# Two token pairs projected from centred rows, loads in another order, and a new order of all steps

## The chip, the cores and the metric

The kernel runs on one core of a Trainium2 chip. The metric is the device time of one execution in microseconds (us), lower is better. The kernel before took 153.5 us (median of 3 runs, 153.39 to 153.69). The profile is of one further execution of 153.96 us.

## The reference, cut to what matters

The input x has 2048 tokens of 448 features. It is layer-normed once, and two branches that read the result are added to x:

```python
xn = _layernorm(x)                       # (x - mean) / sqrt(var + 1e-5), no weights
return x + _A_ref(xn, ...) + _B_ref(xn, ...)

# A: linear attention with a softmax feature map, 16 heads of 28
q, k, v = split(xn @ wqkv)
phi(t) = concat[softmax(t @ w_phi), softmax(-(t @ w_phi))]        # per head, 56 features
kv = sum_s phi(k)^T v ;  z = sum_s phi(k)
o  = (phi(q) @ kv) / (phi(q) @ z + 1e-6) ;  A = o @ wo
# B: feed-forward, 448 -> 1792 -> 448
h = xn @ w1 + b1 ;  B = (h * tanh(softplus(h))) @ w2
```

The norm's scale, 1/sqrt(var + eps), is one number for each token, so a projection of x - mean can be scaled by it afterwards.

## The kernel before, in words

**Tiling.** 2048 tokens are 16 tiles of 128 (t = 0 to 15), and two tiles make a pair u (0 to 7). A pair's normed rows are transposed into xnT (features on partitions); 448 features are three chunks of 128 and one of 64, and the 64 of both tiles share a chunk. `pair_part` splits a projection of a pair into three parts of matmuls on half the array's rows: A (6), B (6) and H (2). A pair of PSUM banks is held from a step's first part to the end of its evacuation; there are four pairs.

**Stages.** Loads; statistics of each tile (`st`, on VectorE by bn_stats, on ScalarE by three activations); the rstd (`rt`, `rs`); normed rows (`xn`, `ln_tile`); their transposes (`xt`, on TensorE or as a DMA transpose in SP's queue). The weights of k and q are first multiplied with w_phi: `wtk` transposes the k weights on TensorE and evacuates them to WT, `wmk` multiplies them to Wpk; the q weights come already transposed by four DMA transposes (`lqT`), `qd` doubles their last 64 columns on VectorE, and `wmq` multiplies them to Wpq. For each pair there is then a k, v and q projection (L429 for all). ScalarE takes exp of k and of q with both signs (L609, L682); v is copied out by ScalarE or VectorE (L509, L511). `kn` normalizes k's features (a sum and a reciprocal on VectorE, a multiplication on GpSimd, L621). `kv` (L650) sums over all pairs, and `kvz` sends the result through a DMA transpose. `e` turns exp(q) of a tile by a DMA transpose in SP's queue, `nd` (L723) makes numerator and denominator, `ot` turns the quotient, `wo` (L845) projects it. The feed-forward is `f` (L429, with Mish on ScalarE, L703) and `g` (L828). VectorE adds x, and the rows are stored.

**What sets the order.** A list of step names, ORDER, written out by hand. `run_order` calls the steps in that order, and each appends its instructions to its engines' programs. So an engine runs its instructions strictly in list order, and an instruction that waits holds up all behind it on that engine, a DMA in SP's or ScalarE's queue too. `resolve` puts in the semaphore waits. `warm` (`z`) issues matmuls of zeros.

Of the kernel before, what the change touches and what calls it, by code (L numbers as in the profile page):

```python
# [38 lines left out]
class Program:  # L39
# [113 lines left out]
v6Aa xn11p kn0.1 k6H v6Ha k3A kn0.0 xt5m kn1.1 l1ms k6A v3Ad kc3 k6B v3Hd k7A v3Bd k7H v4Hd kn6.0 e3 v4Ad k7B v4Bd k4B
v7Ba k4H k4A e2 k5B kn7.1 v7Aa kn7.0 q4H k5A v7Ha kc2 e0 k5H q4A e5 f0.0B q4B f0.0H v5Bd f0.0A e9 f0.8H f0.8A v5Ad
kn5.0 f0.3B f0.8B v5Hd f0.3A e1 f0.4B f0.3H e8 q3B f0.4A f0.5A f0.4H f0.5H f0.2H f0.2A kn1.0 f0.5B kn4.1 q5H e4 q5A
f0.2B q3H kn6.1 loa q7B q5B q7A q7H kn5.1 kn4.0 kv2 kv6 ep kv1 kv0 kv5 kv7 kv4 kv3 q3A f1.0B kvz f0.9A e10 f1.0A f1.0H
e14 f0.9H e15 f0.6A f0.9B f0.7B f0.6H nd0 f0.7A f0.6B f0.11H f0.11A f0.7H f0.10B nd3 f0.11B f0.12A f0.10A e11 e6
f0.10H nd1 f0.12H e7 ot0m f0.1B f0.12B f0.1A f0.1H q6A q6H f1.13H nd2 q6B f1.5A f1.13A f1.4A f1.13B f1.5H f1.1H f1.1A
f1.4B f1.1B f1.5B f1.6A f1.6H e12 f1.4H ot1m f1.11A f1.6B f1.11B nd4 f1.12H f1.11H l2s f1.12A f0.13B f1.12B f1.7A nd5
f1.7H f0.13H f0.13A f1.2H f1.7B ot2m f1.2A nd7 wo0H f1.2B wo1B wo0A wo1A nd6 ot3m wo1H wo0B nd10 g2 g7 g3 g1 g0 nd12  # L160
e13 f1.10A f1.10H f1.9A f1.9H wo3B f1.10B nd13 f1.9B wo3A wo3H f1.8B ot6m f1.3H nd11 f1.3A ot5m g6 g5 f1.8H nd15 f1.8A
wo2H f1.3B sto1 wo2B nd14 nd9 wo2A nd8 g4 sto3 g14 g9 sto2 g12 ot7m g8 ot4m g13 wo7H wo4B wo7A wo5A wo6A wo5H wo6H
# [9 lines left out]
def _kernel(es, nc, A_x, A_wqkv, A_w_phi, A_wo, B_w1, B_b1, B_w2, out):  # L172
    def sb(name, shape, dtype):
        return es.enter_context(nc.sbuf_tensor(name, shape, dtype))
# [108 lines left out]

    def load_qT(g, eng):
        dma(eng, lambda e: e.dma_start_transpose(WqT[:, g, 0:D], A_wqkv[:, g * GP:g * GP + P]), w=[("WqT", g)],
# [618 lines left out]
    add("kvz", kvz)
    add("wob", last_weights)
    add("table", table)
    for eng, c in (("SP", "s"), ("ACT", "a")):
        for a in range(NT):
            for b in range(a + 1, NT + 1):
                add(f"lx{a}.{b}{c}", load_x, a, b, eng)  # L910
        for i, (n, t) in enumerate((("k", Wk), ("v", Wv))):
            add(f"l{n}m{c}", load_main, eng, "W" + n, t, A_wqkv[:, (i + 1) * D:(i + 2) * D])
        add(f"lkt{c}", load_tail, eng, "Wkv", Wkv, A_wqkv[:, D:3 * D])
# [66 lines left out]
```

## Time and profile before

| | us |
|---|---|
| median of 3 runs | 153.5 |
| the profiled execution | 153.96 |
| its span | 152.2 |
| outside the span | 1.76 |
| TensorE busy in the span | 144.6 |
| VectorE, ScalarE, GpSimd busy | 101.1, 75.7, 44.3 |

The page gives the busy time of each engine, the span in 40 slices, and the chain of work that ended last. The timeline gives single instructions with their start and duration; instructions of a group overlap, so a group of n can be shorter than n single ones. "Us to landing" of a DMA is from its issue until its data is there.

### The profile page before, as it was taken

How to read it: one execution, taken by the hardware profiler on the slowest of the kernel's cores; microseconds unless marked ns; L12 is line 12 of the kernel's file. 1: busy time of each engine (PE TensorE's matmuls, PEld its weight loads, DVE VectorE, ACT ScalarE, POOL GpSimd, SP SyncE). 2: the span in 40 equal slices, each digit the busy share in tenths (PEclk: the TensorE clock that was granted, in tenths of full speed). 3: DMA queues.
4: the chain of work that ended last, by engine and by line, in shares of the span. 5: the costliest groups of instructions: out<-in, count | busy, mean ns of one | idle time of the engine just before them, and what ended most of it. 6: DMA issues, size and time to landing. Idle time of an engine off the chain costs nothing.

```text
span 152.2 us, 3611 instructions
## 1 busy us (share of the span) xinstructions
PE 144.6 (95%) x1541; PEld 76.1 (50%) x1541; DVE 101.1 (66%) x223; ACT 75.7 (50%) x90; POOL 44.3 (29%) x65
## 2 busy tenths in 40 slices
PE   3978999989999979999999999999999999999993
PEld 1454545445444574445344455554544554559552
DVE  0699989599969903599606999535995999200721
ACT  3485999995995699778997730000500400000000
POOL 3385688969999950000000000000000000000000
PEclk9999999999999999999999999999999999999999
DMA  5995964989967243994399260500035000540204
GB/s 123 288 260 147 174 143 93 131 268 262 101 137 138 76 139 73 180 197 41 60 149 321 86 65 14 119 0 0 2 65 151 30 4 0 121 121 4 87 4 151
DMA packets 40436, 17.22 MB, mean 113 GB/s; under 512 B 34020, under 2 KB 39908, under 8 KB 40420
## 3 DMA queue, kind: packets, MB, share of 16 engines
q1 hardware_dynamic: 37548, 14.46, 46.9%
q10 hardware_dynamic: 2872, 2.53, 5.6%
q8 instruction: 12, 0.20, 0.5%
q14 instruction: 4, 0.03, 0.1%
HBM read 7.02 MB, written 1.84 MB: 58 GB/s over the span
## 4 chain that ended last, share of the span: by engine, by line
PE 78%; ACT 12%; DMA 4%; DVE 3%; issue 1%; ACTq 0%
PE PS L429 38%; PE PS L828 28%; PE PS L845 7%; DMA x_all<-in_A_x_dram 4%; ACT actT L609 3%; PE PS L723 2%; PE PS L650 2%; ACT actT L682 2%; ACT v_all L509 2%; DVE Sk L627 1%; ACT Wpq L509 1%; ACT Eq L682 1%; DVE v_all L511 1%; ACT Eq L509 1%; ACT Wpk L509 1%
## 5 line engine op out<-in xcount | busy, mean ns | idle before, releaser
L703 ACT ACTIVATE actT<-PS,b1T 128x1024 bf16<-128x1024 f32 x28 | 30.2, 1112 | 33.1 <-PE PS L429 33.0
L429 PE MATMUL PS<-xnT,W 64*128 64x512 bf16 x392 | 46.2, 376 | 0.0
L828 PE MATMUL PS<-W,actT 128*128 128x448 bf16 (+1 forms) x224 | 42.7, 351 | 0.0
L828 PEld LDWEIGHTS PS<-W,actT 128*128 128x128 bf16 x224 | 21.5, 98 | 20.3 <-issue 0.7
L429 PEld LDWEIGHTS PS<-xnT,W 64*128 64x128 bf16 x392 | 18.1, 94 | 21.0 <-ACT actT L703 0.4
L793 DVE TENSOR_TENSOR x_all<-PS,x_all 128x448 bf16<-128x448 f32 (+1 forms) x16 | 9.5, 616 | 20.3 <-PE PS L845 10.3
L621 POOL TENSOR_TENSOR actT<-actT,rSk 128x896 bf16<-128x896 bf16 x12 | 20.0, 1699 | 0.0
L609 ACT ACTIVATE actT<-PS 128x896 bf16<-128x896 f32 x16 | 13.7, 950 | 3.7 <-DVE stats L466 1.8
L429 PE MATMUL PS<-Wkv,xnT 64*128 64x448 bf16 x112 | 13.6, 349 | 0.6 <-DVE v_all L511 0.6
L429 PE MATMUL PS<-Wpk,xnT 64*128 64x448 bf16 x112 | 13.3, 349 | 0.5 <-ACT Wpk L509 0.5
L429 PE MATMUL PS<-Wpq,xnT 64*128 64x448 bf16 x112 | 12.7, 350 | 0.0
L466 DVE BATCH_NORM_STATS2 stats<-x_all 128x6 f32<-128x448 bf16 x15 | 9.2, 614 | 5.2 <-DMA x_all<-in_A_x_dram 5.2
L617 DVE TENSOR_REDUCE Sk<-actT 128x32 f32<-128x896 bf16 x12 | 12.5, 1043 | 0.0
L738 DVE COPY Sq<-PS 128x16 f32<-128x16 f32 x32 | 4.0, 167 | 12.5 <-PE PS L723 12.2
L749 DVE TENSOR_TENSOR xn<-v_all,rden 128x448 bf16<-128x448 f32 x16 | 10.0, 625 | 1.3 <-DMA Wkv<-xn 0.8
L746 DVE TENSOR_TENSOR v_all<-v_all 128x464 f32<-128x464 f32 x16 | 10.3, 642 | 0.6
L742 DVE TENSOR_TENSOR v_all<-PS,Sq 128x464 f32<-128x464 f32 x16 | 10.3, 642 | 0.5
L744 DVE TENSOR_TENSOR v_all<-PS,Sq 128x464 f32<-128x464 f32 x16 | 10.1, 630 | 0.0
L429 PEld LDWEIGHTS PS<-Wkv,xnT 64*128 64x128 bf16 x112 | 5.4, 94 | 6.0 <-DVE v_all L511 1.0
L682 ACT ACTIVATE actT<-PS 128x896 bf16<-128x896 f32 x10 | 8.4, 926 | 0.0
L429 PEld LDWEIGHTS PS<-Wpk,xnT 64*128 64x128 bf16 x112 | 5.3, 94 | 5.5 <-ACT Wpk L509 0.6
L429 PEld LDWEIGHTS PS<-Wpq,xnT 64*128 64x128 bf16 x112 | 5.1, 94 | 5.4 <-ACT actT L609 0.5
(85 smaller groups left out, 137.7 us busy)
## 6 DMA issues: line engine op xcount, KB each, us to landing
W<-in_B_w_dram SPq DMA_DIRECT2D x1, 1568.0 KB, 8.0
out_dram<-x_all SPq DMA_DIRECT2D x7, 224.0 KB, 2.2
W<-in_B_w_dram SPq DMA_DIRECT2D x1, 1344.0 KB, 7.2
x_all<-in_A_x_dram ACTq DMA_DIRECT2D x5, 224.0 KB, 4.1
Wo<-in_A_wo_dram ACTq DMA_DIRECT2D x2, 336.0 KB, 3.6
x_all<-in_A_x_dram SPq DMA_DIRECT2D x2, 224.0 KB, 4.9
W<-in_B_w_dram SPq DMA_DIRECT2D x2, 224.0 KB, 4.0
Wkv<-in_A_wqkv_dram SPq DMA_DIRECT2D x1, 336.0 KB, 4.2
```

The lines of the kernel that those rows point to most:

```text
L429: ins = e.matmul(o, lhs(c, k), rhs(c, k), start=first and n == at[par][0], stop=last and n == at[par][-1])
L609: op("ACT", lambda e, s=s: e.activation(E_of(u)[:, s, :, :], two(b, D), ACT.Exp, scale=1.0 if s == 0 else -1.0), r=[pb(b), pb(b + 1)], w=[ ...
L617: op("DVE", lambda e: e.tensor_reduce(Sk[u][:, s, :], Eh(), AX.X, ALU.add), r=[("E", u, s)], w=[("Sk", u, s)], tag=f"Sk{u}.{s}")
L621: op("POOL", lambda e: e.tensor_tensor(Eh(), Eh(), ap_on(rSk[u][:, s, 0:1], [[1, 2 * H], [0, DH]]), ALU.mult), r=[("E", u, s), ("rSk", u, ...
L682: op("ACT", lambda e, s=s: e.activation(Eq_of(u)[:, :, s, :].rearrange("p i (h n) -> p i h n", n=64)[:, :, :, 0:QP], two(b, D).rearrange(" ...
L703: op("ACT", lambda e: e.activation(actT[:, q, fc, :], bank(b, 2), ACT.Mish, bias=b1T[:, fc:fc + 1]), r=[("b1T",), pb(b), pb(b + 1)], w=[(" ...
L742: op("DVE", lambda e: e.tensor_tensor(tv(t1[i]), num(0), sx(1), ALU.mult), r=[pb(b), pb(b + 1), ("Sq", i, 1)], w=[("t1", i)], tag=f"ta{t}")
L744: op("DVE", lambda e: e.tensor_tensor(tv(t2), num(1), sx(0), ALU.mult), r=[pb(b), pb(b + 1), ("Sq", i, 0)], w=[("t2",)], tag=f"tb{t}")
L746: op("DVE", lambda e: e.tensor_tensor(t1[i], t1[i], t2, ALU.add), r=[("t1", i), ("t2",)], w=[("t1", i)], tag=f"tc{t}")
L749: op("DVE", lambda e: e.tensor_tensor(o_sb[(t // 2) % 2][:, t % 2, :].rearrange("p (h d) -> p h d", d=DH), t1[i][:, :, 0:DH], ap_on(rden[i ...
L828: ins = e.matmul(bank(b)[:, 0:width(t)], act_of(fc, t), W2[:, fc, 0:width(t)], start=first and fc == 0, stop=last and fc == FC - 1)
L845: ins = e.matmul(bank(b)[:, 0:w], oT_of(u)[lo:hi, cc * P:(cc + 1) * P], Wo[lo:hi, cc, 0:w], start=first and n == at[par][0], stop=last and ...
```

## The change

**Centred pairs.** Pairs 0 and 2 are no longer normed before their k, v and q projections. `center` writes x - mean into xc, `center_T` transposes that on TensorE into xR (both live in parts of EqT that are written late). `v_early` copies v out of PSUM times rstd; `k_early` and `q_early` take exp with a scale of rstd or -rstd (`minus_rstd`), one tile at a time, so four pieces of 448 columns instead of two of 896. Both pairs are still normed and turned later, by DMA transposes, for the feed-forward. These projections therefore need the mean of a tile early and its rstd only at the evacuation.

**Loads.** Tiles 0 and 1 come in one load of SP's queue, 4 and 5 first in ScalarE's; the k weights move to ScalarE's queue; the small w_phi loads, which wait for GpSimd's clearing of Wbd, move from ScalarE's queue to SP's, and behind them in SP's queue stand the v weights, tiles 2, 3, 6 and 7 and then the q weights. The last 64 rows of the k weights are loaded once, not twice, and are doubled as `wtk1` is evacuated.

**GpSimd's start.** Three clearings of pads (`pp`) now stand ahead of the zeros and of Wbd.

**Zero products.** 8 (`z7`, `y1.1`) at the start instead of 12, and 4 and 3 more at the very end.

**Order.** All steps are in a new order. Of k, v and q the first are now v and k of pairs 0 and 2; seven of the eight v are copied out by ScalarE (four before). The end has the same kinds of steps in another sequence.

TensorE's program from its start to the first of the q projections: first before, then after. EqT holds the centred rows and their transposes, Wkv the k and v weights, Wbd the w_phi blocks, and Eq the transposed k weights.

```order
L370 MATMUL PS<-zeros 128x512 x12
L547 MATMUL PS<-ident,Wkv 112x128 x16
L504 MATMUL PS<-ident,xn 128x128 x7
L571 MATMUL PS<-Wbd,Eq 128x112 x16
L695 MATMUL PS<-ident,b_rows 128x14
L504 MATMUL PS<-ident,xn 128x128 x7
L429 MATMUL PS<-Wpk,xnT 128x448 x22
L429 MATMUL PS<-Wkv,xnT 128x448 x28
L571 MATMUL PS<-Wbd,WqT 128x112 x16
L429 MATMUL PS<-Wpk,xnT 128x448 x12
```

```order
L390 MATMUL PS<-zeros 128x512 x8
L524 MATMUL PS<-ident,EqT 128x128 x7
L791 MATMUL PS<-ident,b_rows 128x14
L568 MATMUL PS<-ident,Wkv 112x128 x12
L568 MATMUL PS<-ident,Wkv 112x64 x4
L524 MATMUL PS<-ident,EqT 128x128 x7
L598 MATMUL PS<-Wbd,Eq 128x112 x16
L449 MATMUL PS<-Wkv,EqT 128x448 x28
L449 MATMUL PS<-Wpk,EqT 128x448 x10
L598 MATMUL PS<-Wbd,WqT 128x112 x16
L449 MATMUL PS<-Wpk,EqT 128x448 x12
```

The v projections of two pairs now come ahead of k, and the q weights' product (L571 before, L598 after, with WqT) comes after 38 matmuls of projections instead of 50.

SP's queue from its start, before and after; the four DMA_TRANSPOSE of WqT are the q weights.

```order
L273 DMA x_all<-in_A_x_dram 128x448
L276 DMA Wkv<-in_A_wqkv_dram 128x3x448
L281 DMA Wkv<-in_A_wqkv_dram 64x896 x2
L273 DMA x_all<-in_A_x_dram 128x896
L303 DMA b_rows<-in_B_b_dram 14x128
L285 DMA_TRANSPOSE WqT<-in_A_wqkv_dram 128x448 x4
L516 DMA_TRANSPOSE xnT<-xn 128x7x128
```

```order
L287 DMA x_all<-in_A_x_dram 128x896
L323 DMA b_rows<-in_B_b_dram 14x128
L319 DMA Wbd<-in_A_w_phi_dram 28x4x28 x4
L290 DMA Wkv<-in_A_wqkv_dram 128x3x448
L287 DMA x_all<-in_A_x_dram 128x896 x2
L304 DMA_TRANSPOSE WqT<-in_A_wqkv_dram 128x448 x4
L287 DMA x_all<-in_A_x_dram 128x896 x3
L536 DMA_TRANSPOSE xnT<-xn 128x7x128 x5
```

The q weights now stand behind nine loads instead of six, and four of the nine wait for GpSimd. On VectorE the doubling of the q weights (L308) stands, after, directly ahead of the norming of tile 3:

```order
L308 COPY WqT<-WqT 128x4x64
L512 TENSOR_SCALAR xn<-x_all,mv,rstd 128x64
L512 TENSOR_SCALAR xn<-x_all,mv,rstd 128x384
L506 SCALAR_TENSOR_TENSOR shift<-mv,rstd 128x1
L654 TENSOR_SCALAR nrstd<-rstd 128x2
L506 SCALAR_TENSOR_TENSOR shift<-mv,rstd 128x1 x3
L531 CAST Wpq<-PS 128x2x4x56 x2
```

So the rows of pair 1, and two of the four evacuations of Wpq, are queued behind the wait for the q weights.

The diff, cut (of ORDER only the first line of each):

```diff
 ORDER = """
-pi lx1.2a pw table lx0.1s lx4.6a lx2.4a zero st1d lpa st5a st0d st4d st2d rs0p lvma rs2p lx6.8a xn0a xn1d lkms xn5p
+table lx4.6a lkma lx0.2s pp st1d lkta zero lvta pw xc1d st0a xc0d st4d z7 y1.1 st5a pi lbs lps xc5d lvms ct0a b1
...
+    nrstd = sb("nrstd", [P, 8], FP32)
...
+    XR, XC = (15, 14, 13, 12), (11, 10, 9, 8)
+    def flat_of(t):
+        return EqT[:, t, :, :].rearrange("p c n -> p (c n)")[:, 0:7 * P]
+    def xR(u):
+        return flat_of(XR[u]).rearrange("p (c n) -> p c n", n=P)
...
+    def load_kv_tail(i, eng):
+        lo, hi = HALF[i]
+        dst, src = (Wv, A_wqkv[384:448, 2 * D:3 * D]) if i else (Wkv, A_wqkv[384:448, D:3 * D])
+        dma(eng, lambda e: e.dma_start(dst[lo:hi, 3, :], src), w=[("Wt", i)], tag=f"ldWt{i}")
...
-                    ins = e.transpose(oT(c)[:, g, :], Wk[:, 2 * h + c, g * GP:(g + 1) * GP], ident[:])
+                    n = 64 if h and c else P
+                    ins = e.transpose(oT(c)[:, g, 0:n], Wk[0:n, 2 * h + c, g * GP:(g + 1) * GP], ident[0:n, 0:n])
...
+    def center(t, eng):
+        u = t // 2
+        for n, (lo, hi, at) in enumerate([(0, D, 0)] if t % 2 == 0 else [(384, D, D), (0, 384, D + 64)]):
+            src, dst = x_all[:, t, lo:hi], flat_of(XC[u])[:, at:at + hi - lo]
+            op(eng, lambda e, src=src, dst=dst: e.tensor_scalar(dst, src, mv[:, t, 0:1], 0.0, op0=ALU.subtract, op1=ALU.add),
+               r=[("x", t), ("mean", t)], w=[("xc", u, t % 2, n), ("EqT", XC[u])], tag=f"xc{t}.{n}")
+    def center_T(u, eng):
...
+        b = take1()
+        pe(lambda e: transpose7(e, b, flat_of(XC[u])), r, [pb(b)], f"cT{u}")
+        evac(eng, lambda: flat_of(XR[u]), lambda: bank16(b)[:, 0:7 * P], [pb(b)], [("xR", u), ("xRU", u)] + home, f"cTE{u}")
+    def minus_rstd(u):
+        op("DVE", lambda e: e.tensor_scalar(nrstd[:, 2 * u:2 * u + 2], rstd[:, 2 * u:2 * u + 2], -1.0, 0.0, op0=ALU.mult, op1=ALU.add),
...
+    def v_early(u, part, eng):
+        def then(b):
+            for i in range(2):
...
+                    op("ACT", lambda e, dst=dst, src=src, t=t: e.mul(dst, src, rstd[:, t:t + 1]), r=r, w=w, tag=f"vs{u}.{i}")
...
+    def k_early(u, part):
+        def then(b):
+            for s in range(2):
+                for i in range(2):
+                    t = 2 * u + i
+                    op("ACT", lambda e, s=s, i=i, t=t: e.activation(E_of(u)[:, s, i, :], bank(b + i)[:, 0:D], ACT.Exp,
+                                                                    scale=sign_rstd(t, s)),
...
+    def q_early(u, part):
...
+    for i in range(8):
+        for n in range(1, 5):
+            add(f"y{i}.{n}", warm, n)
```

More of the change, by code (lines that the diff above doesn't have):

```diff
@@ L153 @@
[L153 to L162, printed above, removed]
@@ L244, in _kernel, with early_of @@
                  "Wp1": [("Wp", 1, h, c) for h in range(2) for c in range(2)]}
+    XR, XC = (15, 14, 13, 12), (11, 10, 9, 8)
[3 more added lines that the diff above has]
+        return flat_of(XR[u]).rearrange("p (c n) -> p c n", n=P)
+    def early_of(t):
+        return [(n, XR.index(t)) for n in ("xR", "xRU")] if t in XR else \
+            [("xc", XC.index(t), i, n) for i in range(2) for n in range(2 if i else 1)] if t in XC else []
     def oT_of(u):
@@ L292, in rows_of @@
     def rows_of(name):
-        return [(name, 0), ("Wt", 0), ("Wt", 1)] if name in ("Wk", "Wv") else [(name, i) for i in range(3)]
+        return [(name, 0), ("Wt", 0)] + ([("Wt", 1)] if name == "Wv" else []) if name in ("Wk", "Wv") else \
+            [(name, i) for i in range(3)]
     def load_phi(eng):
@@ new lines, in minus_rstd, with sign_rstd @@
+    def minus_rstd(u):
+        op("DVE", lambda e: e.tensor_scalar(nrstd[:, 2 * u:2 * u + 2], rstd[:, 2 * u:2 * u + 2], -1.0, 0.0, op0=ALU.mult, op1=ALU.add),
+           r=[("rstd", 2 * u), ("rstd", 2 * u + 1)], w=[("nr", u)], tag=f"nr{u}")
+    def sign_rstd(t, s):
+        return nrstd[:, t:t + 1] if s else rstd[:, t:t + 1]
+    def v_early(u, part, eng):
+        def then(b):
+            for i in range(2):
+                t = 2 * u + i
+                dst, src = v_all[:, u, i, :, 0:DH], bank(b + i)[:, 0:D].rearrange("p (h d) -> p h d", d=DH)
+                r, w = [pb(b + i), ("rstd", t)], [("v", u)] if i else [("vh", u)]
+                if eng == "ACT":
+                    op("ACT", lambda e, dst=dst, src=src, t=t: e.mul(dst, src, rstd[:, t:t + 1]), r=r, w=w, tag=f"vs{u}.{i}")
+                else:
+                    op("DVE", lambda e, dst=dst, src=src, t=t: e.tensor_scalar(dst, src, rstd[:, t:t + 1], 0.0, op0=ALU.mult,
+                                                                               op1=ALU.add), r=r, w=w, tag=f"vs{u}.{i}")
+        pair_part(f"v{u}", part, tok_works(u, Wv, True), x_res(u, True) + rows_of("Wv"), then)
@@ new lines, in k_early @@
+    def k_early(u, part):
+        def then(b):
+            for s in range(2):
+                for i in range(2):
+                    t = 2 * u + i
+                    op("ACT", lambda e, s=s, i=i, t=t: e.activation(E_of(u)[:, s, i, :], bank(b + i)[:, 0:D], ACT.Exp,
+                                                                    scale=sign_rstd(t, s)),
+                       r=[pb(b + i), ("rstd", t), ("nr", u)], w=[("E", u, s)] if i else [("Eh", u, s)], tag=f"exkc{u}.{s}.{i}")
+        pair_part(f"k{u}", part, tok_works(u, Wp[1], True),
+                  x_res(u, True) + [("Wp", 1, h, c) for h in range(2) for c in range(2)], then)
@@ new lines, in q_early, with then @@
+    def q_early(u, part):
+        def then(b):
+            for s in range(2):
+                for i in range(2):
+                    t = 2 * u + i
+                    op("ACT", lambda e, s=s, i=i, t=t: e.activation(
+                        Eq_of(u)[:, i, s, :].rearrange("p (h n) -> p h n", n=64)[:, :, 0:QP],
+                        bank(b + i)[:, 0:D].rearrange("p (h n) -> p h n", n=QP), ACT.Exp, scale=sign_rstd(t, s)),
+                       r=[pb(b + i), ("Eqp", u % 3), ("rstd", t), ("nr", u)], w=[("Eq", u % 3, s)],
+                       tag=f"exqc{u}.{s}.{i}")
+        pair_part(f"q{u}", part, tok_works(u, Wp[0], True), x_res(u, True) + [("Wp", 0, c) for c in range(4)], then)
@@ L903, in _kernel @@
                 add(f"f{q}.{fc}{part}", ffn1, q, fc, part)
+    for u in range(4):
+        add(f"nr{u}", minus_rstd, u)
+        for eng, c in (("ACT", "a"), ("DVE", "d"), ("both", "b")):
+            add(f"ct{u}{c}", center_T, u, eng)
+        for part in "ABH":
+            add(f"v{u}{part}e", v_early, u, part, "ACT")
+            add(f"v{u}{part}f", v_early, u, part, "DVE")
+            add(f"k{u}{part}c", k_early, u, part)
+            add(f"q{u}{part}c", q_early, u, part)
+        for t in (2 * u, 2 * u + 1):
+            add(f"xc{t}d", center, t, "DVE")
+            add(f"xc{t}p", center, t, "POOL")
     add("kvz", kvz)
@@ L912, in _kernel @@
             add(f"l{n}m{c}", load_main, eng, "W" + n, t, A_wqkv[:, (i + 1) * D:(i + 2) * D])
-        add(f"lkt{c}", load_tail, eng, "Wkv", Wkv, A_wqkv[:, D:3 * D])
+        for i, n in enumerate("kv"):
+            add(f"l{n}t{c}", load_kv_tail, i, eng)
         add(f"l1m{c}", load_main, eng, "W1", W1, B_w1)
```

58 lines of the change are left out of this document (44 added, 14 removed).

## The prediction

> **What bounds the kernel now.** I read the page first, then the busy time by stage, the chain of waits, and the timeline of the first 20 us. The page:
>
> ```profile
> span 152.2 us, 3611 instructions
> ...
> PE 144.6 (95%) x1541; PEld 76.1 (50%) x1541; DVE 101.1 (66%) x223; ACT 75.7 (50%) x90; POOL 44.3 (29%) x65
> ...
> PE 78%; ACT 12%; DMA 4%; DVE 3%; issue 1%; ACTq 0%
> ```
>
> TensorE (PE) is busy for 95% of the span, and the chain is mostly its. Where is it not dense? The windows view, with TensorE's busy time as the second number, for all that comes after the kv sum:
>
> ```profile
> 57.10:149.25 92.15, 92.15 (x931) 48.05 (x928) 56.35 (x129) 31.59 (x30) 0.11 (x1) 1.00 0.38 81
> ```
>
> There it never waits. The change issues the same matmuls there in another order, so nothing is to be won there. The chain (start, duration, what) shows the rest:
>
> ```profile
> 1.74 5.48 DMA x_all<-in_A_x_dram
> ...
> 11.06 0.81 ACT Wpk L509
> ...
> 11.92 4.17 PE PS L429 x42
> ...
> 33.20 0.96 DVE v_all L511
> ...
> 34.21 18.73 PE PS L429 x184
> ...
> 56.10 0.78 issue
> ```
>
> The first projection starts at 11.92 us. From there TensorE is without work only at 34.2 (0.6 us, the row below) and at 56.1 (0.78, where no engine is waited for). So I count with one equation: the end is the first projection's start, plus 152.2 - 11.92 = 140.3 us, plus new waits of TensorE, less the waits that go.
>
> ```profile
> PE PS L429 <- DVE v_all L511: 0.6, 1, 0.6
> ```
>
> **When the first projection starts.** The timeline of before prices each link (start, duration):
>
> ```profile
> 3.63 0.63 DVE L466 BATCH_NORM_STATS2 stats<-x_all 128x6 f32<-128x448 bf16 x1 [3.63 <-DMA x_all<-in_A_x_dram]
> ...
> 5.42 0.58 ACT L458 ACTIVATE junk<-x_all 128x448 bf16<-128x448 bf16 x1 [2.87 <-DMA x_all<-in_A_x_dram]
> ...
> 6.92 0.19 ACT L462 ACTIVATION_READ_ACCUMULATOR junk<-x_all,rmean 128x1 f32 x1
> ...
> 8.06 0.58 DVE L492 TENSOR_SCALAR xn<-x_all,mv,rstd 128x64 bf16<-128x64 bf16 x2
> ...
> 8.84 1.00 ACT L509 ACTIVATE Eq<-PS 112x1024 bf16<-112x1024 bf16 x1
> ...
> 9.90 0.96 PE L571 MATMUL PS<-Wbd,Eq 112*128 112x112 bf16 x16 [0.34 <-ACT Eq L509]
> ...
> 10.96 0.90 ACT L509 ACTIVATE Wpk<-PS 128x896 bf16<-128x896 f32 x1
> ```
>
> The arrival of data, from the DMA issues (the last number is us to landing) and the windows (the last is GB/s):
>
> ```profile
> x_all<-in_A_x_dram SPq DMA_DIRECT2D x1, 112.0 KB, 2.6
> x_all<-in_A_x_dram ACTq DMA_DIRECT2D x1, 112.0 KB, 2.8
> ```
>
> ```profile
> 2.00:3.00 1.00, 0.69 (x2) 0.28 (x3) 0.00 (x0) 0.54 (x1) 0.25 (x2) 1.00 1.01 221
> 3.00:4.00 1.00, 1.00 (x4) 0.32 (x3) 0.37 (x1) 0.00 (x0) 0.00 (x0) 1.00 0.96 295
> ```
>
> Tiles 0 and 1 now come in one load of 224 KB, beside 224 KB of tiles 4 and 5. At 221 KB by 3 us and 295 KB per us from there, 448 KB are there at 3.8. The bounds are 3.4, as before, and 4.4; I take 3.9. VectorE then needs about 1.8 us (statistics of tile 1, 0.63 and a short second step, and two centrings at 0.58 and less), and TensorE has turned pair 0 by 6.5. But ScalarE runs in list order: statistics of tiles 0 and 5 (5.42 to 7.11 before, so 1.69 each: to 7.3), pair 0's transpose (0.90: to 8.2), half of the k weights' second evacuation (half of 1.00: to 8.7), pair 2's transpose (0.90: to 9.6). The second half of the k weights' product (half of 0.96) follows the 8.7 and stands on TensorE directly ahead of the first v part, which so starts at 9.2; its third part needs the 9.6. With a few tenths for handovers I take **9.6 us, 2.3 earlier** (bounds 9.1 and 10.5, with the arrival's). Wpk, two evacuations later at 11.4, is wanted only at 12.3.
>
> The v weights must be there too. SP's queue issues the tile load, the biases and then waits for GpSimd, which starts at 0.81 and now clears three pads ahead of Wbd; after the four w_phi loads follow the v weights:
>
> ```profile
> 1.69 0.53 POOL L333 MEMSET Wbd<- 112x512 bf16 x1
> ...
> 2.28 1.95 ACTq L299 DMA_DIRECT2D Wbd<-in_A_w_phi_dram  x4
> ...
> 4.09 5.10 SPq L285 DMA_TRANSPOSE WqT<-in_A_wqkv_dram  x4
> ...
> 10.50 0.56 POOL L341 MEMSET actT<- 128x256 bf16 x2
> ```
>
> ```profile
> Wkv<-in_A_wqkv_dram ACTq DMA_DIRECT2D x1, 336.0 KB, 3.8
> ```
>
> Pads 3 x 0.28, zeros 0.1, Wbd 0.53: cleared at 2.3. Four loads in 1.95 put the v weights' issue at 4.3, landing at 8.1. The cover is 1.5 us; without it, each microsecond is one of the end.
>
> **The q weights.** After 28 matmuls of v and 10 of k, TensorE reaches the q weights' product:
>
> ```profile
> 2.31 5.03 PE L370 MATMUL PS<-zeros 128*128 128x512 bf16 x12 [2.31 <-POOL zeros L322]
> ...
> 14.01 2.81 PE L429 MATMUL PS<-Wkv,xnT 64*128 64x448 bf16 x28
> ...
> 15.01 0.23 DVE L289 COPY WqT<-WqT 128x256 bf16<-128x256 bf16 x1
> ```
>
> That is 9.6 + 38 x 0.095 (2.7 for 28, less the overlap at the end) = 13.2. The four transposing loads of the q weights were issued from 4.09, one per 1.28. Now three more issues at 0.49 stand behind the w_phi loads, so they begin at 5.7, the last at 9.6. Times to landing: all four as smallest, median, largest, then the median of the last two.
>
> ```profile
> DMA to landing us min/median/max: 3.7/4.6/5.4
> ```
>
> ```profile
> WqT<-in_A_wqkv_dram SPq DMA_TRANSPOSE x2, 4.2
> ```
>
> With 4.2 they are there at 13.8, doubled by VectorE (0.23) at 14.1: **a new wait of 0.9** (0.3 with 3.7, 2.0 with 5.4). It holds up all of TensorE's queue. On VectorE it holds up the rows of tile 3 and two evacuations of Wpq, and through tile 3 SP's transpose of pair 1:
>
> ```profile
> xnT<-xn SPq DMA_TRANSPOSE x6, 3.8
> ```
>
> Tile 3 is normed at 14.6, pair 1 turned at 18.4. TensorE wants it after the product (0.9) and 32 matmuls (3.1), at 18.1. **0.4** for this and the Wpq evacuations (0 to 1.2).
>
> **ScalarE, GpSimd and W1.** ScalarE gets more work between 14 and 43 us. Four early k and q steps take four pieces of 448 instead of two of 896, and three more v are copied out there:
>
> ```profile
> 17.72 1.86 ACT L509 ACTIVATE Wpq<-PS 128x448 bf16<-128x448 f32 x4
> ...
> 19.41 3.40 ACT L609 ACTIVATE actT<-PS 128x896 bf16<-128x896 f32 x4
> ```
>
> ```profile
> L609 ACT ACTIVATE actT<-PS 128x896 bf16<-128x896 f32 x16 | 13.7, 950 | 3.7 <-DVE stats L466 1.8
> ```
>
> 4 x (1.86 - 1.70) + 3 x 0.85 = 3.2 us more, against 3.7 us that it idled ahead of the exps of k. It just fits, so I cost it at nothing; TensorE runs two to three steps ahead of it on four pairs of banks. The copy at 34.2 that made TensorE wait moves from VectorE to ScalarE: **0.6 won** (0 to 0.6). GpSimd's sixteen multiplications for the kv sum:
>
> ```profile
> 27.11 5.01 POOL L621 TENSOR_TENSOR actT<-actT,rSk 128x896 bf16<-128x896 bf16 x3
> ...
> 45.03 9.99 POOL L621 TENSOR_TENSOR actT<-actT,rSk 128x896 bf16<-128x896 bf16 x6
> ```
>
> They end at 55.02, and the last kv step started at 56.88, so they may begin 1.9 us later before anyone waits. W1 moves from SP's to ScalarE's queue behind the v copy of pair 5, near 30 by the count of projections ahead of it:
>
> ```profile
> W<-in_B_w_dram SPq DMA_DIRECT2D x1, 1344.0 KB, 7.2
> ```
>
> It lands near 37.2, for a first f part near 38.5 by the same count, and shares the engines with pair 6's transpose: **0.2** (0 to 2). The zero products at the end (7 x at most 0.42) lie behind the last matmul, beside the last stores, which take the 2.95 us from 149.25 to the end: nothing.
>
> **The sum.** -2.3 + 0.9 + 0.4 - 0.6 + 0.2 = -1.4. The profiled execution's 153.96 us (span 152.2 and 1.76 around it) become 152.6. The median of the runs, 153.5, is 0.46 below that execution; the same step gives **152.1 us**.
>
> **A rule against it: the clock.** The twelve zero products took 0.42 each, but the projections 0.095 per half-array matmul, so 0.19 for a pair of 448 columns, or 0.22 scaled to 512: TensorE ran at half rate until about 7.2 us, 4.9 after its first product, though the page's granted clock reads full throughout. Now there are eight products, over at 5.2, and a gap of 0.5 before the first transpose. If the gap restarts the 4.9 us, full rate comes at 10.6: the transposes and the product ahead of v run at half, and v starts near 10.5. That is 0.9 lost. The Trainium skill, "TensorE: Matmul & The Clock Gate", Part 1, says that full rate comes after a busy window of about 3.4 us, that the window runs freely and that it goes only after an idle one of that length. By that rule the shorter warm-up can miss a window (an estimate from its figure: up to 3.4 us of half rate, 1.7 lost), but a gap of 0.5 alone throws nothing away; the 0.42 agrees with its cold rate, and no run yet shows the window.
>
> **Rivals.**
> - *Forecast* (45%): 151.3 to 152.9.
> - *The lead is larger* (14%): the q weights land before 13.2 and nothing else waits: -2.3 - 0.6 = -2.9, 150.6. For it: a landing of 3.7 leaves only 0.3 of the wait. Against it: nine issues stand ahead of them in SP's queue.
> - *Clock* (11%): -1.4 + 0.9 = -0.5: 153.0, and 152.6 to 153.5 with the bounds.
> - *Given back to the q weights* (12%): a landing of 5.4 makes the wait 2.0 and the one for pair 1 0.4 (tile 3 normed at 15.8, turned at 19.6, wanted at 19.2): -2.3 - 0.6 + 2.0 + 0.4 + 0.2 = -0.3: 153.2, no change. For it: DMA moves some 300 GB/s at that time, so a landing is late when more is under way.
> - *Slower* (18%): ScalarE becomes the bound from 14 to 43 us. A piece of 448 may not overlap the next (different scale, strided output), and then costs 0.57 instead of 0.465, the mean of the row below: 16 x 0.1 = 1.6 more. And of the 3.7 us of idle time, the 1.8 in its row fell near 14 us, where ScalarE now waits again, for the q weights. 3.2 + 1.6 - 1.9 = 2.9 us by which its evacuations free the banks late: -1.4 + 2.9 = +1.5: 155.0. It decides from 1.4 us of such lateness on. Against it: four pairs of banks, and TensorE two to three steps ahead.
>
> ```profile
> L509 ACT ACTIVATE Wpq<-PS 128x448 bf16<-128x448 f32 x4 | 1.9, 568 | 0.0
> ```
>
> A measurement here can tell about 0.2% (0.3 us) from no change. Faster by more: the forecast, the larger lead and most of the clock case, 0.69. Within: the given-back case and the rest of the clock's, 0.13. Slower: 0.18. The range reaches from 150.6 to 154.2: it leaves out half of the slower case and half of the larger lead.
>
> **What would show it.** Right: the first projection (L449, Wkv<-EqT) at 9.6 (9.1 to 10.5); TensorE idle ahead of L598 with WqT by 0.3 to 2, released by VectorE's L308; no wait at 34; TensorE dense to the end after kv. Wrong: zero products and transposes at half rate behind 7 us (clock); TensorE waiting for ScalarE's L705 or L778 between 18 and 45 (given back); a wait at L598 of 2.5 or more; a wait for W1 or pair 6 near 33 to 39; a kv step that waits for GpSimd's L717.

## The result and the profile after

The changed kernel took 160.36 us (median of 4 executions, 159.14 to 161.87), beside 153.56 for the kernel before (153.39 to 153.69) on the same chip. The ratio is 1.039 (95% interval 1.034 to 1.044): slower by 6.8 us, where 152.1 was forecast and 154.2 was the upper end. Medians below are over all executions of a kernel; the intervals of ratios leave out executions over 1.5% above its fastest one, so where times spread widely only the times are used.

The profiled execution took 160.43 us. Its page, with the clock of TensorE by slices:

```profile
span 159.0 us, 3646 instructions
...
PE 150.0 (94%) x1544; PEld 78.6 (49%) x1544; DVE 98.6 (62%) x227; ACT 80.6 (51%) x102; POOL 48.3 (30%) x69
...
PEclk9999999999599999999999999999999999999999
...
PE 69%; ACT 10%; DMA 7%; DVE 7%; POOL 5%; issue 1%; POOLq 0%
```

TensorE's share is still 94%, so its share alone says nothing of 6.8 us lost. Two things do: one slice with half the clock, and DMA with 7% of the chain instead of 4%. The windows of after, cut at the first projection, at the places where TensorE stops and comes back, behind the kv sum and shortly before the last matmuls end (second number: TensorE busy):

```profile
11.49:36.00 24.51, 23.79 (x241) 11.67 (x240) 21.13 (x59) 22.31 (x38) 19.36 (x28) 1.00 0.84 152
36.00:40.65 4.65, 0.16 (x2) 0.03 (x1) 3.19 (x6) 1.41 (x2) 3.35 (x3) 0.97 1.13 306
40.65:64.92 24.27, 24.16 (x320) 13.28 (x320) 11.26 (x16) 21.03 (x23) 16.74 (x12) 0.94 0.44 85
64.92:155.80 90.88, 90.88 (x917) 46.92 (x914) 56.45 (x129) 28.55 (x27) 0.24 (x1) 1.00 0.38 87
```

After the kv sum it never waits, as forecast. The loss sits between 36.0 and 40.65. TensorE's timeline names what it waited for:

```profile
6.02 0.91 PE L524 MATMUL PS<-ident,EqT 128*128 128x128 bf16 x7 [0.72 <-DVE EqT L635]
...
11.49 3.56 PE L449 MATMUL PS<-Wkv,EqT 64*128 64x448 bf16 x28
...
35.24 0.92 PE L449 MATMUL PS<-Wkv,xnT 64*128 64x448 bf16 x8
40.65 1.30 PE L449 MATMUL PS<-Wkv,xnT 64*128 64x448 bf16 x6 [4.49 <-DMA xnT<-xn]
```

The last row is the first v part of pair 6. Its normed rows come by a DMA transpose in SP's queue (L536). The issues in SP's queue (start, duration), with that of W1's main part in ScalarE's (L290, ACTq) between them by time; two transposes of other pairs are left out:

```profile
26.12 1.23 SPq L786 DMA_TRANSPOSE EqT<-actT  x1
...
31.18 1.24 SPq L295 DMA_DIRECT2D W<-in_B_w_dram  x2
32.17 0.39 ACTq L290 DMA_DIRECT2D W<-in_B_w_dram  x1
32.51 1.25 SPq L536 DMA_TRANSPOSE xnT<-xn  x1
```

The DMA view of 32.5 to 40.5 us (the last column of an issue is us to landing), then that of 35 to 36 us, where q1 is SP's queue and q10 ScalarE's (packets, MB, share of the time of 16 engines):

```profile
W<-in_B_w_dram ACTq DMA_DIRECT2D x1, 1344.0 KB, 7.5
...
xnT<-xn SPq DMA_TRANSPOSE x1, 8.0
```

```profile
q10 hardware_dynamic: 92, 0.33, 95.7%
q1 hardware_dynamic: 5, 0.00, 0.3%
```

W1 was issued 0.34 us ahead of the transpose of pair 6. The transpose landed 8.0 us after its issue, where the transposes of the kernel before took 3.8 (median). While both were under way W1's queue had nearly all of the engines' time: from 34.5 to 38 us it had 95.7%, and SP's queue 6.7%. The transpose landed 0.8 us after W1. The Trainium skill, "DMA: Bandwidth & Descriptors", section "Queues, rings and completion order", says that each DMA engine takes turns between the queues that have work for it, a packet at a time. With 97 packets of SP's queue beside 327 of W1's in that stretch the trace does not show even turns; whether SP's queue had work for every engine all that time no run here tells.

After the wait TensorE ran at half rate (the granted clock is the third number from the end):

```profile
40.00:41.00 1.00, 0.35 (x3) 0.18 (x5) 1.00 (x2) 0.00 (x0) 1.00 (x2) 0.66 1.29 265
41.00:42.00 1.00, 1.00 (x8) 0.49 (x6) 0.55 (x2) 0.00 (x0) 1.00 (x1) 0.50 1.24 273
42.00:43.00 1.00, 1.00 (x8) 0.49 (x6) 0.00 (x0) 0.00 (x0) 1.00 (x2) 0.50 1.06 197
43.00:44.00 1.00, 1.00 (x10) 0.47 (x7) 0.00 (x0) 0.52 (x1) 1.00 (x1) 0.63 1.07 210
```

These windows count 8 to 10 matmuls in a full us, where 34 to 35 and 44 to 45 us count 14 and 15. The loss is the missing share of the clock times the busy time: 0.34 x 0.35 + 0.5 + 0.5 + 0.37 = 1.5 us.

The account of the 6.8 us (span 159.0 against 152.2):

| | us |
|---|---|
| first projection at 11.49, not 11.92 | -0.43 |
| TensorE idle behind it: 0.72 + 4.49 + 0.11, against 45.18 - 43.81 = 1.37 before | +3.95 |
| half rate in the first v projections: 3.56 against 2.81 | +0.75 |
| half rate behind the wait | +1.49 |
| from the end of the last matmul that isn't a zero product (156.30, before 149.75) to the span's end | +0.25 |
| the rest: TensorE's busy time for the other matmuls is longer, spread over many places | +0.8 |

### The profile page after: what moved, and what is told of

Read it like the earlier page. It is cut to its first block, busy times and chain, and to the rows that moved or that the text cites. A ratio compares the mean times of both kernels' runs of the same rounds, so it can differ in the third digit from the quotient of the medians.

```text
span 159.0 us, 3646 instructions
## 1 busy us (share of the span) xinstructions
PE 150.0 (94%) x1544; PEld 78.6 (49%) x1544; DVE 98.6 (62%) x227; ACT 80.6 (51%) x102; POOL 48.3 (30%) x69
## 3 DMA queue, kind: packets, MB, share of 16 engines
q10 hardware_dynamic: 1392, 2.45, 4.7%
## 4 chain that ended last, share of the span: by engine, by line
PE 69%; ACT 10%; DMA 7%; DVE 7%; POOL 5%; issue 1%; POOLq 0%
PE PS L449 28%; PE PS L924 27%; PE PS L941 7%; DMA xnT<-xn 5%; ACT actT L778 3%; ACT actT L799 3%; PE PS L819 2%; DVE Sk L713 2%; DMA x_all<-in_A_x_dram 2%; PE PS L746 2%; POOL rstd L495 2%; DVE xn L512 1%; DVE stats L486 1%; PE PS L598 1%; POOL EqT L635 1%
## 5 line engine op out<-in xcount | busy, mean ns | idle before, releaser
L449 PE MATMUL PS<-xnT,W 64*128 64x512 bf16 x392 | 45.3, 376 | 0.0
L717 POOL TENSOR_TENSOR actT<-actT,rSk 128x896 bf16<-128x896 bf16 x14 | 23.4, 1697 | 5.5 <-DVE rSk L715 5.5
L713 DVE TENSOR_REDUCE Sk<-actT 128x32 f32<-128x896 bf16 x14 | 14.6, 1039 | 5.9 <-ACT actT L705 5.9
L449 PE MATMUL PS<-Wkv,xnT 64*128 64x448 bf16 x84 | 11.3, 381 | 4.5 <-DMA xnT<-xn 4.5
L449 PE MATMUL PS<-Wpk,xnT 64*128 64x448 bf16 x84 | 10.5, 362 | 0.4 <-ACT Eq L689 0.4
L705 ACT ACTIVATE actT<-PS 128x896 bf16<-128x896 f32 x12 | 10.5, 989 | 0.0
L840 DVE TENSOR_TENSOR v_all<-PS,Sq 128x464 f32<-128x464 f32 x16 | 10.1, 630 | 0.0
L449 PE MATMUL PS<-Wpq,xnT 64*128 64x448 bf16 x84 | 10.0, 349 | 0.0
L449 PEld LDWEIGHTS PS<-Wkv,xnT 64*128 64x128 bf16 x84 | 4.3, 99 | 9.2 <-issue 5.9
L529 ACT ACTIVATE v_all<-PS 128x896 bf16<-128x896 f32 x5 | 4.9, 985 | 6.6 <-PE PS L449 6.6
L518 POOL TENSOR_SCALAR xn<-x_all,rstd,shift 128x448 bf16<-128x448 bf16 (+2 forms) x12 | 7.5, 633 | 1.7 <-DVE shift L506 1.7
```

Of the source, the lines that this page charges most:

```text
L449: ins = e.matmul(o, lhs(c, k), rhs(c, k), start=first and n == at[par][0], stop=last and n == at[par][-1])
L705: op("ACT", lambda e, s=s: e.activation(E_of(u)[:, s, :, :], two(b, D), ACT.Exp, scale=1.0 if s == 0 else -1.0), r=[pb(b), pb(b + 1)], w=[ ...
L713: op("DVE", lambda e: e.tensor_reduce(Sk[u][:, s, :], Eh(), AX.X, ALU.add), r=[("E", u, s)], w=[("Sk", u, s)], tag=f"Sk{u}.{s}")
L717: op("POOL", lambda e: e.tensor_tensor(Eh(), Eh(), ap_on(rSk[u][:, s, 0:1], [[1, 2 * H], [0, DH]]), ALU.mult), r=[("E", u, s), ("rSk", u, ...
L840: op("DVE", lambda e: e.tensor_tensor(tv(t2), num(1), sx(0), ALU.mult), r=[pb(b), pb(b + 1), ("Sq", i, 0)], w=[("t2",)], tag=f"tb{t}")
```

## The experiments

Theory: with W1 in ScalarE's queue, a transposing load of SP's queue that is under way beside it is held up until W1 is in, and pair 6 is wanted before that. The rivals are in the expectations. In the list of steps, `l1ma` loads W1's main part from ScalarE's queue, `l1ms` from SP's, `xt6m` is the transpose of pair 6, and `e2` turns exp(q) of a tile in SP's queue.

**1. W1 behind the transpose, in one queue.**

```diff
-... k4B v4Aa l1ma k4H xn12p l1ts k7B kn0.1 v4Ha k4A xt6m v7Aa ...
+... k4B v4Aa k4H xn12p l1ts k7B kn0.1 v4Ha k4A xt6m l1ms v7Aa ...
```

> The changed kernel with one step moved: W1's main load (1.34 MB) leaves ScalarE's queue and stands in SP's queue directly behind the transpose of pair 6. Theory (W1 in the way: both move at once, so that the transpose takes 8.0 us instead of 3 to 4, TensorE waits 4.5 us and then runs at half rate for 3 us): the transpose is issued near 32.5 as before the move and lands by 36.5, TensorE waits under 1 us, no half rate near 41, 154.5 to 155.5. Rival (the transpose is late only because SP's queue stood behind the turn of tile 2): W1 makes no difference, the landing stays above 6 us, 159 to 161. If W1 itself is now late for the first f part, TensorE waits there by 0 to 1.5 us.

Measured: 153.91 (median of 10, 153.14 to 156.72), beside 154.0 for the kernel before on that chip: ratio 0.999 (0.996 to 1.002). The timeline and, for 30 to 34 us, the DMA issues:

```profile
30.19 1.25 SPq L536 DMA_TRANSPOSE xnT<-xn  x1
31.48 0.59 SPq L290 DMA_DIRECT2D W<-in_B_w_dram  x1
```

```profile
W<-in_B_w_dram SPq DMA_DIRECT2D x1, 1344.0 KB, 6.6
...
xnT<-xn SPq DMA_TRANSPOSE x1, 3.8
```

Nothing else was changed. This execution had an earlier start, so W1 was issued 0.7 us earlier and the transpose 2.3, and both came sooner: the transpose in 3.8, W1 in 6.6. There was no wait for pair 6 and no half rate near 41, and the time lies below the 154.5 to 155.5 expected. This one line of the change is the whole slowdown: without it the kernel is level with the one before. What the rest of the change is worth cannot be read from that, since W1's new place has a price of its own (experiment 5).

**2. The transpose of pair 6 earlier**, with the turn of exp(q) that stood ahead of it (issued at 26.12 above) moved behind it.

```diff
-... v3Ha e2 k5B ... xt6m v7Aa v7Ha e4 ...
+... v3Ha k5B ... xt6m v7Aa v7Ha e2 e4 ...
```

> The changed kernel with one step moved: the turn of tile 2 (waits for ScalarE's exp of pair 1's q) no longer stands in SP's queue ahead of the transposes of pairs 4, 7 and 6, but behind them. W1 stays in ScalarE's queue. Theory (W1 in the way): the transpose of pair 6 is issued near 30 instead of 32.5, most of it is through before W1 starts at 32.2, TensorE waits under 1 us, 154 to 155.5. Rival (the place in SP's queue does not matter because the rows of pairs 7 and 6 are ready late): issue still near 32, wait of over 3 us, 159 to 161.

Measured: 161.03 (median of 10), from 154.24 to 164.96: four executions at 154.2 to 156.0 (three of them in the 154 to 155.5 expected), six at 159.4 to 165.0. The profiled one took 164.01:

```profile
44.41 1.30 PE L449 MATMUL PS<-Wkv,xnT 64*128 64x448 bf16 x6 [10.20 <-DMA xnT<-xn]
```

```profile
W<-in_B_w_dram ACTq DMA_DIRECT2D x1, 1344.0 KB, 14.1
xnT<-xn SPq DMA_TRANSPOSE x1, 14.7
```

The transpose was issued at 29.54, 3 us earlier than in the changed kernel and 0.7 ahead of W1, and landed later, at 44.2, with W1 at 44.3. So in this execution neither a late issue nor standing behind W1 in time is the cause: what they share is the time in flight. Why the executions of this kernel differ so much stays open; only this one of them has a profile.

**3. TensorE kept busy through the wait**, by zero products ahead of pair 6's first v part: 16 in one kernel, 40 in another. The lines are those of the 40; the 16 are `y2.4 y3.4 y5.4 y6.4` in the same place.

```diff
-... v7Aa v7Ha e4 v6Aa ...
+... v7Aa v7Ha z16 z16 z8 e4 v6Aa ...
```

> The changed kernel with 16 zero products (3.5 us at full rate) put ahead of the part of v of pair 6 at which TensorE waits. They add work only inside the wait. Theory (the half rate from 40.2 to 43.5 comes from TensorE's idleness): it goes, 1.3 to 1.7 us faster than the changed kernel, 158.5 to 159. Rival (the matmuls there are slow for another reason, W1's and the transposes' traffic): the half rate stays, 160 to 161.

> The changed kernel with 40 zero products (8.6 us at full rate) ahead of the v part of pair 6 at which TensorE waits; the time is that of a kernel with more work and says nothing, the rate of the first matmuls behind is read. Theory (idleness brings the half rate): with TensorE at work through most of the wait, six v matmuls take 0.73 us, not 1.30, unless it still idled for 3.5 us or more. Rival (they are slow for the traffic): 1.30 again.

With 16: 156.54, 160.63, 163.45, and one of 547.6 that nothing here explains. The products were over at 37.7, pair 6 landed at 42.9, and after 5.2 us without work TensorE came back at half rate, so that kernel decides nothing. With 40 (one execution, 161.46) they covered the landing at 39.6. First the row of the kernel with 16, then those of the kernel with 40:

```profile
42.92 1.30 PE L449 MATMUL PS<-Wkv,xnT 64*128 64x448 bf16 x6 [5.22 <-DMA xnT<-xn]
```

```profile
34.31 8.93 PE L390 MATMUL PS<-zeros 128*128 128x512 bf16 x40
...
43.17 0.74 PE L449 MATMUL PS<-Wkv,xnT 64*128 64x448 bf16 x6
```

The six matmuls take 0.74 instead of 1.30, and the clock reads 1.00, while the DMA share from 43.17 to 44 us is 1.22, as high as in the changed kernel's half rate: the half rate behind the wait comes from the idle time, not from the DMA traffic. The products ran on for 3.6 us after the landing, so nothing was won by them.

**4. A better start alone**: twelve zero products again instead of eight.

```diff
-... st4d z7 y1.1 st5a ...
+... st4d z12 st5a ...
```

> The changed kernel with 12 zero products at the start instead of 8. Theory (8 products with a gap behind them do not bring TensorE to full rate, and the half rate until 13 us costs about 1.9 us of transposes and products on the way to the first v part and 0.7 in it): transposes and products from 7 on at full rate, the first v part near 10.3, and, as ScalarE's exps and W1's issue shift along, 158 to 159.5 in all. Rival (the start is bound by ScalarE's statistics and GpSimd's centring): first v part later than 11, 160 to 161.

Measured: 160.53 (159.63 to 161.5, 4 executions), ratio 1.043 (1.036 to 1.050). The first projection started at 10.15, 1.3 us earlier than in the changed kernel and as the theory had it, but the 158 to 159.5 did not come: all of the gain went into the wait:

```profile
40.54 1.30 PE L449 MATMUL PS<-Wkv,xnT 64*128 64x448 bf16 x6 [6.31 <-DMA xnT<-xn]
```

With W1 and the transpose as they are, the end is set by their landing. An earlier start only issues both earlier (30.14 and 30.30), and they take 9.7 and 10.1.

**5. Both edits, and the best combination.** The fifth kernel is 1 and 4 together. The sixth also centres tile 4 on VectorE instead of GpSimd, loads tiles 14 and 15 from SP's queue behind the first transpose, and leaves out the zero products at the end.

```diff
-lx2.4s pk rs0p lx6.8s xc4p ... xt1m xn4p ... wmq1d lx14.16a ... g15 y0.4 sto6 sto4 y4.3 stt15
+lx2.4s pk rs0p lx6.8s xc4d ... xt1m lx14.16s xn4p ... wmq1d ... g15 sto6 sto4 stt15
```

> The changed kernel with W1's main load in SP's queue behind the transpose of pair 6, and 12 zero products at the start instead of 8. Theory (once nothing waits for pair 6, what is left between the executions is the moment at which TensorE reaches full rate, and 12 products bring it there in every execution): executions closer together than with W1 moved alone (153.1 to 156.7), median 153.0 to 153.9. Rival (the spread there comes from DMA traffic, not from the clock): the same spread, same median 153.9.

> As the run with W1 moved and 12 zero products, and three more edits: VectorE centres tile 4 instead of GpSimd (1.8 us there); the load of tiles 14 and 15 leaves ScalarE's queue, where it ran beside the transpose of pair 1 (6.0 us to landing), and stands in SP's queue behind it; no zero products at the end. Theory (a transpose that runs beside a plain load of the other queue is late, and the first v part is bound by the slower of ScalarE's chain and GpSimd's centring): first v part at 9.4 to 9.8 instead of 10.15, pair 1 lands within 4.5 us, the wait of 0.9 for it goes: 1.0 to 1.8 us faster, 152.0 to 152.9, faster than the kernel before. Rival (ScalarE bounds the stage up to 45 us): the start moves, the end does not: 153.5 to 154.

The fifth took 154.04 (153.36 to 154.66), beside 153.86 before: 1.0015 (0.9996 to 1.0034). It spreads less than the first experiment's, as expected, but its median is no better. The sixth took 153.49 (152.24 to 154.33): 0.9987 (0.996 to 1.001), no difference that can be told, where 152.0 to 152.9 was expected. Pair 1 landed in 4.2 and its wait went, as expected. Its profiled execution happened to be the fastest, 152.24 with a span of 150.5. Two further executions show what differs.

> The best combination again, one look, to see what differs between executions of one kernel (152.2 to 154.3 in the ten runs). Theory (the start of the first projection varies with the moment at which full rate is granted): if the time is above 153.2, the first projection starts 0.8 to 1.5 later than the 9.5 of the profile at 152.24, with transposes at half rate. Rival (the landing of the transposes varies): the start is 9.5 to 9.8, and the difference is waits for xnT between 13 and 40.

> As the look before: one more profile of the best combination, with the same two readings of it.

The two further executions took 153.65 and 152.76. The first projection started at 9.54, 9.41 and 9.21, so the start does not vary with the time, against the theory; nor did TensorE wait for xnT in any of the three, against the rival. The difference lies later. In the execution of 153.65 (in that of 152.76 the same wait was 0.5, in the fastest there was none):

```profile
43.33 2.87 PE L449 MATMUL PS<-xnT,W 64*128 64x512 bf16 x24 [1.15 <-ACT actT L778]
```

L778 is ScalarE's exp of q. The first of these exps, of pair 4, writes the buffer that held pair 1's, and so needs the turn of tile 3 (`e3`) to be done. That turn now stands in SP's queue behind W1. Its row, first in the fastest execution, then in the one of 153.65 (the named matmuls had long been done):

```profile
40.16 3.35 ACT L778 ACTIVATE actT<-PS 128x896 bf16<-128x896 f32 x4 [0.15 <-PE PS L449]
```

```profile
41.55 3.35 ACT L778 ACTIVATE actT<-PS 128x896 bf16<-128x896 f32 x4 [1.60 <-PE PS L449]
```

The landings of the issues from 30 to 36 us, in the same order:

```profile
W<-in_B_w_dram SPq DMA_DIRECT2D x1, 1344.0 KB, 6.7
EqT<-actT SPq DMA_TRANSPOSE x2, 7.3
```

```profile
W<-in_B_w_dram SPq DMA_DIRECT2D x1, 1344.0 KB, 7.5
EqT<-actT SPq DMA_TRANSPOSE x2, 8.1
```

So the load of W1 still makes transposes late, other ones, with more slack. The turn of tile 3 landed at 40.09, 40.59 and 41.48 in the executions of 152.24, 152.76 and 153.65, and the exp started 0.07 us later in each. In the profiles of experiment 1 and of the fifth kernel it landed at 41.62 and 42.53. In all five the time of the whole execution is that landing plus 112.1 to 112.2 us: with W1 in this place, the turn behind it sets the end. No run moved that turn, so what the kernel would take without this wait is not shown.

**6. The same collision in the kernel before.** Its W1 stands in SP's queue behind the last transpose. Two kernels move it to ScalarE's queue at about the same time (first), and much earlier, when pairs 3 and 6 are being turned (second).

```diff
-... v6Ha k3A kn0.0 xt5m kn1.1 l1ms k6A ...
+... v6Ha l1ma k3A kn0.0 xt5m kn1.1 k6A ...
```

```diff
-... wmq1a wmq0a k2A rt12p ... xt5m kn1.1 l1ms k6A ...
+... wmq1a wmq0a k2A l1ma rt12p ... xt5m kn1.1 k6A ...
```

> The kernel before with one step moved: W1's main load leaves SP's queue, where it stands behind the last transpose of normed rows, and goes to ScalarE's queue behind the v copy of pair 6, issued near 28 us, some tenths after the last transpose (pair 5). Theory (the order within one queue protects the transpose, another queue does not): the transpose of pair 5 lands after 7 us or more instead of 3.9, TensorE waits for it near 35 for 0 to 6 us, executions spread by several us, 154 to 160. Rival (the changed kernel is slow there for another reason): same as before, 153.5 to 154.2.

> The kernel before, with W1's main load moved from SP's queue to ScalarE's, behind the copy of pair 0's middle k columns, so issued near 20.3 instead of 28.9. Theory (a transposing load of SP's queue that is in flight beside the load of W1 from ScalarE's queue lands only with it): the transposes of pairs 3 and 6, issued near 19 to 21 and landing after 2.9 in the kernel before, land after 5 to 8; pair 6, wanted at 25.2, comes 1.5 to 4 late; 154.9 to 157.5. Rival (what came late in the changed kernel was pair 6's own place, not the queue of W1): landing 2.9 to 4.9 as before, no wait, 153.4 to 154.2.

The first took 153.68, ratio 0.999 (0.997 to 1.000): the slowdown expected of it did not come. Its DMA issues from 26.5 to 29 us show why that is no case against the theory:

```profile
W<-in_B_w_dram ACTq DMA_DIRECT2D x1, 1344.0 KB, 6.4
xnT<-xn SPq DMA_TRANSPOSE x1, 7.7
```

The transpose of pair 5, issued at 26.73, 0.5 us ahead of W1, was held up to 7.7. But no part of TensorE's program waited for it: that kernel has slack there. The second took 156.53 (156.24 to 157.15), as expected; the ratio is 1.018 (1.014 to 1.022). W1 was issued at 18.55, earlier than expected. The waits, and the issues of 18.5 to 22.5 us:

```profile
26.14 0.74 PE L429 MATMUL PS<-Wpk,xnT 64*128 64x448 bf16 x6 [1.19 <-DMA xnT<-xn]
...
27.37 0.74 PE L429 MATMUL PS<-Wkv,xnT 64*128 64x448 bf16 x6 [0.49 <-DMA xnT<-xn]
```

```profile
W<-in_B_w_dram ACTq DMA_DIRECT2D x1, 1344.0 KB, 6.6
xnT<-xn SPq DMA_TRANSPOSE x2, 6.6
```

The same view of the kernel before:

```profile
xnT<-xn SPq DMA_TRANSPOSE x2, 2.9
```

The transposes of pairs 3 and 6 took 6.9 and 6.2 instead of 2.9, and TensorE waited 1.7 for them, of 2.4 us between the two profiled executions. The theory holds in the other kernel, with nothing of the change's order in it.

**7. The changed kernel with W1 only after pair 6.** W1 stays in ScalarE's queue, behind the copy of pair 6's first v columns.

```diff
-... v4Aa l1ma k4H ... v6Aa e3 k7H ...
+... v4Aa k4H ... v6Aa l1ma e3 k7H ...
```

> The changed kernel, with the load of W1 still in ScalarE's queue but behind the copy of pair 6's first v columns, so that it is issued only when pair 6 has been used (near 37.3). Theory: pair 6 lands 3 to 4.5 after its issue at 32.5 and TensorE waits for it 0 to 0.8; W1 is then late for the first f part (wanted near 40.5, there at 44 to 45): the wait moves to W1, 3 to 4.5, with half rate behind it; 157 to 159.5. Rival (pair 6 is late by its own place in SP's queue, behind the load of W1's last columns and pair q1's transpose): pair 6 lands after 7 to 8 as in the changed kernel, W1 is issued near 42 and lands near 49; 164 to 167.

Measured: 155.62 (154.8 to 160.0, 6 executions), ratio 1.009 (1.004 to 1.013). The issues of 31.5 to 36 us, and the row of the first f part:

```profile
W<-in_B_w_dram ACTq DMA_DIRECT2D x1, 1344.0 KB, 8.7
...
xnT<-xn SPq DMA_TRANSPOSE x1, 3.8
```

```profile
43.72 0.82 PE L449 MATMUL PS<-xnT,W 64*128 64x512 bf16 x6 [1.91 <-issue]
```

Pair 6 came in 3.8, from the same place in SP's queue: its place is not the cause. W1, issued at 34.95, landed near 43.6, and the first f part started then: the wait moved to W1, as the theory has it, but was 1.9 instead of 3 to 4.5, and the time lies below the 157 to 159.5 expected. W1 was issued 2.3 us earlier than expected, and then took 8.7 beside turns of SP's queue.

## Why the prediction was wrong, step by step

**The step that failed** is the term for W1: "It lands near 37.2, for a first f part near 38.5 by the same count, and shares the engines with pair 6's transpose: 0.2 (0 to 2)". The collision was named, also among what would show the prediction wrong ("a wait for W1 or pair 6 near 33 to 39"), but mis-sized. It measured 4.5 us of waiting and 1.5 of half rate behind it: 6.0, three times the upper bound. Without it (experiment 1) the kernel is level with the one before. Two things were left out of the price. One is the nearest row: in the kernel before, between 28.5 and 36 us, the two turns of exp(q) that stood behind W1 in its own queue took as long as W1, and the transpose ahead of it 3.5.

```profile
W<-in_B_w_dram SPq DMA_DIRECT2D x1, 1344.0 KB, 7.2
EqT<-actT SPq DMA_TRANSPOSE x2, 7.5
...
xnT<-xn SPq DMA_TRANSPOSE x1, 3.5
```

With the issue and the need as they were measured, 7.5 us from 32.5 is 40.0, and pair 6 was wanted at 36.0: a wait of 4. The prediction gave its 0.2 without such a row, and of W1's new place worked out only when W1 itself would be wanted. The other is the second price of a long wait: the clock.

**The start** was forecast at 9.6 and measured 11.49. With the clock at full rate the same first stage started at 10.15 (experiment 1). The missing 0.5 goes back to GpSimd's centring of tile 4, for which TensorE waited 1.2 us there; with it on VectorE and twelve products, the three profiled executions of the best combination started at 9.2 to 9.5. So the chain was priced rightly but for one operation that it left out: GpSimd took 1.79 us for these 128 x 448 numbers in the changed kernel, VectorE 0.33 in the best combination.

**The clock rival** (11%, "v starts near 10.5", 0.9 lost) did happen in the profiled execution, and was larger: half rate until about 13.0 (the first 28 matmuls took 3.56 instead of 2.81, so some 1.5 us of them ran at half), a start at 11.49 and 0.75 more in the first v projections. Experiment 4 shows that it cost nothing at the end, since the wait for pair 6 took up whatever the start gained.

**The q weights** (0.9, 0.3 to 2.0): no wait. The doubling ran at 12.68, and the product wanted it at 15.92 in the changed kernel; in the best combination it ran at 12.14 for 13.24. The last of the four loads landed 2.7 us after its issue, where 3.7 was taken as the shortest. **Pair 1** (0.4): no wait in the changed kernel, 0.85 in experiment 1, right in kind. **The wait at 34.2** went, as forecast. **The slower rival**, ScalarE as the bound, did not come: the waits of TensorE for ScalarE add up to 0.6 us in the changed kernel. The slower outcome came by another way, one that I had as a term with too low a bound and not as a rival.

**The sum** would not have held without W1 either: forecast -1.4, and experiment 1, the whole change with W1 behind pair 6, is level. In its profile the first projection starts 1.77 us earlier than in the kernel before, but TensorE took 137.5 us of busy time from its first projection to its last matmul instead of 136.5 for the same matmuls, idled 1.6 instead of 1.4, and 2.8 instead of 2.45 passed behind the last one. So the equation, which took the 140.3 us behind the first projection as fixed but for waits, failed too. Part of it is the turn behind W1 (experiment 5); where the longer busy time comes from is not traced. The best combination, which mends the start as well, gives -1.7 in its fastest execution (152.24 against 153.96) but a median with a ratio of 0.9987, whose interval holds 1.

## What to carry to other kernels

Before a load changes its queue, list the transfers in flight beside it and the time at which each is wanted, and price them by a row of the trace in which such a transfer flew beside such a load, not by its usual time. A big load that is wanted late goes behind the small ones that are wanted early, in the same queue; sent from another queue it held up here even a transpose that was issued 0.5 to 0.7 us ahead of it. What stands behind it in its own queue is late as well, so look there for the next wait. An early gain is worth nothing until the wait that comes last is known: the 1.3 us of a better start vanished whole.

## What was not expected of the hardware

**Two queues could be slower than one for both transfers.** W1 took 6.6 to 7.5 us in SP's queue behind the transpose (five profiles of experiments 1 and 5), and 7.5, 9.7 and 14.1 in its own queue beside it (the changed kernel, experiments 4 and 2); the transpose took 3.8 to 4.2 against 8.0, 10.1 and 14.7. In the kernel before it was only the transposes that were late; W1 took 6.4 and 6.6 there from ScalarE's queue, as against 7.2 from SP's. Why nearly the same program lands them in 8 us or in 14 was not found. The shares differ: W1's queue had 95.7% of the engines' time and SP's 6.7% in the changed kernel (34.5 to 38 us), but 62.7% and 49.8% in experiment 2 (32 to 42 us), where both were slowest.

**The warm-up differs between executions, and a short gap can undo it.** With eight zero products, experiment 1 ran its first transposes at full rate (0.55 for seven) and the changed kernel at half (0.91) until 13.0. In experiment 7 full rate was there, and went in a gap of 1.32 us:

```profile
5.79 0.55 PE L524 MATMUL PS<-ident,EqT 128*128 128x128 bf16 x7 [0.49 <-DVE EqT L635]
8.90 0.93 PE L524 MATMUL PS<-ident,EqT 128*128 128x128 bf16 x7 [1.32 <-POOL EqT L635]
...
11.25 3.23 PE L449 MATMUL PS<-Wkv,EqT 64*128 64x448 bf16 x28
```

Full rate returned within that first v group. In experiment 1 a gap of 1.18 at the same place did no harm, and with twelve products full rate held in all five profiled executions. The Trainium skill, "TensorE: Matmul & The Clock Gate", Part 1, says that the clock is decided over a window of about 3.4 us that runs freely, and that full rate goes after an idle window of that length. The differing starts agree with a free-running window, and the half rate behind 4.5 and 5.2 us of idleness with the length; the loss behind 1.32 us does not, if idleness alone counts. In that execution TensorE ran nothing but transposes from the end of the zero products (5.29) to 8.90, and in experiment 1 from 5.09 to 8.87 without a loss; whether transposes count as work for the clock no run here tells.
